# A fused attention and mixture kernel: split pieces and matrix products placed otherwise among the attention steps

## The chip, the cores and the metric

The kernel runs on one core of a Trainium2 chip. The core has a matrix engine (TensorE, PE in the profile, with PEld for its weight loads), VectorE (DVE), ScalarE (ACT), GpSimd (POOL) and SyncE (SP), which issues nearly all DMAs. The metric is the device time of one execution in microseconds, the median of several runs.

## The reference

Three layers run one after the other: local and global attention, a layer that takes the maximum of three products, and a routed mixture with capacity.

```python
s_ll = scale * np.matmul(q_l, k_l.transpose(0, 1, 3, 2))      # 2 x 8 heads, 512 rows, 64 wide, window 32
...
a_l = sm(s_l)
out_l = np.matmul(a_l, np.concatenate([v_g, v_l], axis=2))
...
h = np.maximum(np.maximum(x @ w1, x @ w2), x @ w3)            # 1088 x 512 by 512 x 768
return (h @ w_out).astype(np.float32)
...
expert_idx = np.argmax(logits, axis=1)                        # 8 experts, capacity 288
```

`w1`, `w2`, `w3` and `w_out` arrive as 64-bit floats.

## The kernel before

The whole program is written in a fixed order: each engine works through its own queue in the order in which the source emits instructions, and waits there for what an instruction needs.

**Attention steps.** The local attention is cut into 32 units (`NU`), two for each of 16 sets of a batch, a half and a head pair. The loop `for s in range(-2, NU + 6)` runs a pipeline: in step s the scores of unit s + 2 are multiplied (L179), their mask and maximum are taken on VectorE (L193) and their exponential on ScalarE (L198); unit s is transposed on TensorE (L212) and copied by ScalarE (`ph`, L217); unit s - 1 is multiplied with the values (L226) and scaled by VectorE (`xq`, L228); unit s - 2 is transposed to its place (`pxq`, L234), copied by ScalarE (`xs`, L237), and split into a high and a low part `xh`, `xl` by GpSimd (L239, L240). The string `SEQ` says in which order a step emits these, and where the letters w0 to w2, m0 to m3 and `idle` stand among them. In every fourth step `g_scores` adds the global queries' scores (L257) and `g_copies` takes them out of PSUM (L272).

**Splitting.** `w_stream` turns each 128 x 512 chunk of 64-bit weights into two float32 parts (`wh`, `wl`). There are 18 chunks for the three weights, six groups f of three, and six of `w_out`. A chunk is loaded by SP into a buffer `raww` (L361), of which there are three. Its pieces, in order, are: absolute value on ScalarE (L337), clamp (L339), shift (L342) and sign merge into `ct` (L345) on VectorE, the cast to `wh` on ScalarE (L349), exponent mask (L352) and low part (L354) on VectorE, and two subtractions and additions on GpSimd (L355, L356). `take(ws, n)` emits n pieces; the table `w_steps` gives the number for each step, a third of it at each w. A chunk has seven takes, and the end of one chunk runs in between the start of the next. `load(k + 2)` is emitted when chunk k - 1 has been finished, into the buffer that it leaves.

**Products of the first layer.** `moe_first(f, c0, T)` gives 36 products (L454) of one window of rows with one group f: three maxima of 12 products. `ORDER` lists window, group and the step from which they may run. `pull(n)` emits n of them; `MM` gives the numbers at m0 to m3, 14 in a step. They begin in step 12. What is left of the listed 432 runs after the loop, and everything behind it is a long stretch of products.

**Unread products.** `warm(n)` multiplies a tile of zeros (L88) into a PSUM bank that nobody reads; `idles` gives n for each step.

**Loads.** In even steps the loop issues the next set's queries and keys (`qk`, L97) and values (`rawv`, L101), five buffers each. SP issues in source order, too, and a load that has to wait for its buffer holds the ones behind it.

## Time and profile before

| what | value |
|---|---|
| median of 3 runs | 327.69 us |
| lowest and highest | 327.64 and 328.4 us |
| the profiled execution's own time | 329.9 us |
| its span, first to last instruction | 328.1 us |
| PE busy | 309.8 us, 94% of the span |
| DVE, ACT, POOL busy | 235.7, 181.3, 148.6 us |
| mean granted TensorE clock | 0.974 |

The profiled execution took 2.2 us more than the median, of which 1.8 us lie outside its span. The profile's page gives busy times, 40 slices of the span, and groups of instructions by source line. A group's line reads: line, engine, operation, output from inputs, shapes, count, busy time and mean duration, then the idle time just before and what ended it. The granted clock 1.00 is 2.4 GHz and 0.50 is 1.2 GHz.

### The profile page before, as it was taken

Reading aid. Unit: us, or ns where it says so; the run is one execution under the profiler, and the core shown is the slowest. Engines: PE = TensorE matmul, PEld = TensorE weight load, DVE = VectorE, ACT = ScalarE, POOL = GpSimd, SP = SyncE. Lnnn points to the kernel's source line nnn. Section 1 sums busy time; section 2 is a strip of 40 time slices with the busy share of each in tenths; the row PEclk is TensorE's granted clock in tenths of the full one; section 3 lists DMA queues with packets and bytes.
Section 4 is the critical chain, followed back from the end, with each engine's and each line's share of the span. In section 5 each row is a group of like instructions: output and inputs, shape, how many; then the busy total and the mean of one; then the engine's idle time right before and its main releaser. Section 6 shows DMA issues by size and latency. Waiting matters only on the chain. (4 is left out here: it accounts for less than half of the span.)

```text
span 328.1 us, 8717 instructions
## 1 busy us (share of the span) xinstructions
PE 309.8 (94%) x3280; PEld 264.3 (81%) x3280; DVE 235.7 (72%) x600; ACT 181.3 (55%) x457; POOL 148.6 (45%) x164
## 2 busy tenths in 40 slices
PE   7699868999999999999999999999899999999993
PEld 2355746778887899999999999999799777788762
DVE  2569988796688827998996001765879799999881
ACT  4668477768757522433443121346532689889860
POOL 1128958593674814676888000142000357831131
PEclk9869796999999999999999999999999999999999
DMA  7947777486253962243310011469756189999921
GB/s 243 413 162 274 262 262 249 160 303 212 80 193 125 193 155 66 66 130 128 130 64 3 0 65 64 146 237 346 231 170 256 53 312 399 395 405 399 390 81 32
DMA packets 27656, 64.43 MB, mean 196 GB/s; under 512 B 3018, under 2 KB 8140, under 8 KB 27600
## 3 DMA queue, kind: packets, MB, share of 16 engines
q1 hardware_dynamic: 26304, 59.91, 52.9%
q0 software_dynamic: 1296, 3.82, 3.1%
q8 instruction: 30, 0.49, 0.6%
q14 instruction: 26, 0.21, 0.2%
HBM read 60.95 MB, written 7.27 MB: 208 GB/s over the span
## 5 line engine op out<-in xcount | busy, mean ns | idle before, releaser
L454 PE MATMUL h<-xh,wh 128*128 128x256 f32 (+1 forms) x288 | 85.3, 296 | 0.5 <-DVE hA L441 0.5
L454 PE MATMUL h<-xl,wh 128*128 128x256 f32 (+1 forms) x288 | 85.5, 297 | 0.0
L454 PE MATMUL h<-xh,wl 128*128 128x256 f32 (+1 forms) x288 | 85.5, 297 | 0.0
L454 PEld LDWEIGHTS h<-xh,wh 128*128 128x128 f32 x288 | 55.6, 193 | 1.2 <-DVE hA L441 0.7
L454 PEld LDWEIGHTS h<-xh,wl 128*128 128x128 f32 x288 | 55.9, 194 | 0.8 <-issue 0.7
L454 PEld LDWEIGHTS h<-xl,wh 128*128 128x128 f32 x288 | 55.9, 194 | 0.4 <-issue 0.2
L444 POOL TENSOR_TENSOR hTl<-hA,hTh 128x256 fp32r<-128x256 f32 (+1 forms) x24 | 19.3, 806 | 55.8 <-ACT hTh L443 55.7
L239 POOL CAST xh<-xs 128x128 fp32r<-128x128 f32 x32 | 13.1, 408 | 37.0 <-ACT xs L237 37.0
L859 DVE TENSOR_TENSOR w2l<-rawb,w2h 128x1024 fp32r<-128x1024 f32 x23 | 27.3, 1214 | 2.0 <-ACT w2h L858 2.0
L443 ACT CAST hTh<-hA 128x256 fp32r<-128x256 f32 (+1 forms) x24 | 10.0, 416 | 33.6 <-DVE hA L441 33.5
L739 PE MATMUL x<-hTl,wo_h 128*128 128x256 f32 (+1 forms) x96 | 28.3, 294 | 0.0
L198 ACT ACTIVATE sm<-sm,nm 128x128 f32<-128x128 f32 x64 | 25.3, 399 | 5.3 <-DVE nm L193 5.2
L441 DVE TENSOR_TENSOR hA<-hA,h 128x256 f32<-128x256 f32 (+1 forms) x48 | 20.7, 432 | 10.3 <-PE h L454 8.5
L739 PE MATMUL x<-hTh,wo_l 128*128 128x256 f32 (+1 forms) x96 | 27.9, 291 | 0.0
L739 PE MATMUL x<-hTh,wo_h 128*128 128x256 f32 (+1 forms) x96 | 27.8, 289 | 0.0
L355 POOL TENSOR_TENSOR ct<-ct,wh 128x512 f32<-128x512 f32 x18 | 25.8, 1432 | 1.3 <-DVE ca L352 0.9
L193 DVE CUSTOM_DVE_ANT_0 sm<-s,mask 128x128 f32<-128x128 f32 x64 | 15.9, 285 | 13.8 <-PE s L179 9.2
L942 PE MATMUL py<-w2h,hhl 128*128 128x512 f32 x96 | 25.5, 395 | 0.2 <-DVE idsall L573 0.2
L356 POOL TENSOR_TENSOR wl<-ct,ca 128x512 fp32r<-128x512 f32 x18 | 24.3, 1352 | 2.0 <-DVE ca L354 0.7
L859 DVE TENSOR_TENSOR w1l<-rawb,w1h 128x1024 fp32r<-128x1024 f32 x20 | 23.7, 1216 | 1.7 <-ACT w1h L858 1.6
L858 ACT CAST w2h<-rawb 128x1024 fp32r<-128x1024 f32 x23 | 23.4, 1050 | 1.8 <-DMA rawb<-in_w_dram 1.8
L817 POOL DMA_INDIRECT xg<-x2d,idsall x7 | 14.8, 2120 | 16.0 <-PE xp L829 14.8
(232 smaller groups left out, 723.3 us busy)
## 6 DMA issues: line engine op xcount, KB each, us to landing
rawb<-in_w_dram SPq DMA_DIRECT2D x51, 512.0 KB
raww<-in_w_dram SPq DMA_DIRECT2D x18, 512.0 KB
rawv<-in_v_dram SPq DMA_DIRECT2D x16, 512.0 KB
qk<-in_qk_dram SPq DMA_DIRECT2D x16, 320.0 KB
rawo<-in_w_out_dram SPq DMA_DIRECT2D x6, 512.0 KB
rw<-in_w_dram SPq DMA_DIRECT2D x5, 512.0 KB
out_dram<-zero SPq DMA_DIRECT2D x1, 2176.0 KB
rawg<-in_vo_dram SPq DMA_DIRECT2D x4, 512.0 KB
```

Source lines behind the costliest of these rows:

```text
L193: nc.vector.tensor_tensor_reduce(sm[:, j], ps[:, j, 0:P], mk, scale=-0.125, scalar=3.0e38, op0=ALU.add, op1=ALU.min, accum_out=nm[:, j : j ...
L198: nc.scalar.activation(sm[:, j], sm[:, j], AF.Exp, bias=nm[:, j : j + 1], scale=-1.0, accum_out=ssum[:, j : j + 1])
L355: nc.gpsimd.tensor_tensor(tf, tf, hi.bitcast(F32), op=ALU.subtract)
L356: nc.gpsimd.tensor_tensor(lo, tf, b.bitcast(F32), op=ALU.add)
L441: nc.vector.tensor_tensor(hA[:, :T], hA[:, :T], ph[:, :T], op=ALU.max)
L444: nc.gpsimd.tensor_tensor(hl[:, f_, c0 : c0 + T], hA[:, :T], dst.bitcast(F32), op=ALU.subtract)
L454: nc.tensor.matmul(ph[:, :T], lhsT=w_[:, a], rhs=x_[:, c, c0 : c0 + T], start=n == 0, stop=n == 11)
L739: nc.tensor.matmul(po[:, :T], lhsT=w_[:, f, d * P : (d + 1) * P], rhs=h_[:, f_, c0 : c0 + T], start=k == 0, stop=k == 17)
L817: nc.gpsimd.indirect_dma_start(out=xg[t if j == 0 else j % 2], out_offset=None, in_=src, in_offset=bass.IndirectOffsetOnAxis(ap=IDS[j][0:n ...
L858: nc.scalar.copy(h_, raw_of(j, k))
L859: nc.vector.tensor_tensor(l_, raw_of(j, k), h_.bitcast(F32), op=ALU.subtract)
L942: nc.tensor.matmul(py[0:nt], lhsT=a[:, c, a0 : a0 + nt], rhs=w_[:, c], start=i == 0, stop=i == 23)
```

## The change

All of it lies in the attention steps and the splitting inside them.

- In `split64` the cast to `wh` changes places with the exponent mask, and a chunk's start has three pieces behind the load instead of four. So the cast now comes behind the absolute value of the next chunk, and the low part one take later. The temporaries `ca` and `ct` get three buffers, `raww` five, and chunk k + 3 is loaded when the low part of chunk k - 1 has been emitted.
- Two weight loads are emitted before the loop, and the sets' loads come one set earlier.
- `w_steps` has 2 to 4 pieces in most steps where it had 1 to 7.
- Before step 17, ten products are emitted in a step (`MM`), and the second group's (f = 1) may run from step 14, 16 and 17, its three maxima apart, where they had to wait for step 17. `moe_stream` no longer emits the first product of an entry under the step of the one before.
- `idles` has 26 unread products where it had 12: four as before in step -2, one in each of steps 0 to 11, two in each of steps 12 to 16.
- Three times (sets 0, 2 and 4), half of the global scores is copied by ScalarE instead of VectorE.

```diff
-            (nc.vector.tensor_copy if m < GDVE else nc.scalar.copy)(SG_[b, hp // 2][64 * j : 64 * j + 64, half * 256 : half * 256 + n], o)
+            (nc.vector.tensor_copy if j == 0 and m < GDVE else nc.scalar.copy)(SG_[b, hp // 2][64 * j : 64 * j + 64, half * 256 : half * 256 + n], o)
...
-        b = wp.tile([P, 512], I32, tag="ca", name="ca")
+        b = wp.tile([P, 512], I32, tag="ca", bufs=3, name="ca")
...
-        t = wp.tile([P, 512], I32, tag="ct", name="ct")
+        t = wp.tile([P, 512], I32, tag="ct", bufs=3, name="ct")
...
+        nc.vector.tensor_scalar(a, t, -0x800000, None, op0=ALU.bitwise_and)
+        yield
+
         nc.scalar.copy(hi, tf)
-        yield
-
-        nc.vector.tensor_scalar(a, t, -0x800000, None, op0=ALU.bitwise_and)
         yield
...
-            raw = wp.tile([P, 512, 2], I32, tag="raww", bufs=3, name=name)
+            raw = wp.tile([P, 512, 2], I32, tag="raww", bufs=5, name=name)
...
             next(old, None)
-            if k:
-                load(k + 2)
             yield
-            for _ in range(4):
+            next(old, None)
+            load(k + 3)
+            yield
+            for _ in range(3):
                 next(new, None)
                 yield
...
-    ORDER = [(0, 0, 12), (0, 1, 17), (1, 1, 19), (1, 0, 18), (1, 2, 21), (2, 1, 27), (0, 2, 25), (2, 2, 31), (2, 0, 32), (3, 0, 99), (3, 1, 99), (3, 2, 99)]
+    ORDER = [(0, 0, 12), (0, 1, (14, 16, 17)), (1, 1, 18), (1, 0, 18), (1, 2, (22, 23, 25)), (0, 2, 25), (2, 1, 27), (2, 2, 31), (2, 0, 32), (3, 0, 99), (3, 1, 99), (3, 2, 99)]
...
-    MM = (7, 4, 2, 1)
+    MM = ((5, 3, 2, 0), (7, 4, 2, 1))
...
     dma_v(1)
+    take(ws, 1)
+    dma_qk(3)
+    dma_v(2)
+    take(ws, 1)
...
-            m = (s + 6) // 2
-            if 3 <= m < NSET:
+            m = (s + 8) // 2
+            if 4 <= m < NSET:
                 dma_qk(m)
```

SP's queue at the start, before the change, from the first weight load on (`raww` chunks, `qk` and `rawv` of the sets; the waits are for landed DMAs and for engines that still read the buffer):

```order
L361 DMA raww_164<-in_w_dram 128x1024 [waits DMAHW0_49]
L361 DMA raww_166<-in_w_dram 128x1024 [waits DMAHW1_49]
L97 DMA qk_211<-in_qk_dram 128x640 [waits DMAHW2_49]
L101 DMA rawv_213<-in_v_dram 128x1024 [waits DMAHW3_49]
L361 DMA raww_254<-in_w_dram 128x1024 [waits DMAHW4_49]
L97 DMA qk_299<-in_qk_dram 128x640 [waits DMAHW5_49]
L101 DMA rawv_301<-in_v_dram 128x1024 [waits DMAHW6_49]
L97 DMA qk_389<-in_qk_dram 128x640 [waits DMAHW7_49,PE_49]
L101 DMA rawv_391<-in_v_dram 128x1024 [waits DMAHW0_49]
L361 DMA raww_485<-in_w_dram 128x1024 [waits DMAHW1_49,DVE_49,Activation_49]
```

The same queue after the change:

```order
L361 DMA raww_149<-in_w_dram 128x1024 [waits DMAHW0_49]
L97 DMA qk_151<-in_qk_dram 128x640 [waits DMAHW1_49]
L101 DMA rawv_153<-in_v_dram 128x1024 [waits DMAHW2_49]
L361 DMA raww_155<-in_w_dram 128x1024 [waits DMAHW3_49]
L97 DMA qk_215<-in_qk_dram 128x640 [waits DMAHW4_49]
L101 DMA rawv_217<-in_v_dram 128x1024 [waits DMAHW5_49]
L361 DMA raww_261<-in_w_dram 128x1024 [waits DMAHW6_49]
L97 DMA qk_307<-in_qk_dram 128x640 [waits DMAHW7_49,PE_49]
L101 DMA rawv_309<-in_v_dram 128x1024 [waits DMAHW0_49]
L361 DMA raww_345<-in_w_dram 128x1024 [waits DMAHW1_49]
```

The fourth set's `qk` stands ahead of the second weight chunk instead of behind it, and the fourth chunk's load no longer waits for VectorE and ScalarE.

ScalarE's queue in steps 9 and 10 before the change; `sm` are a unit's exponentials, `ph` the copied transposes that TensorE multiplies next, `wh` the cast of a weight chunk:

```order
L198 ACTIVATE sm_126,ss_541<-sm_126,nm_595 128x128 [waits DVE_49] x2
L201 ACTIVATE ss_541<-ss_541 128x4 [waits Activation_49]
L349 CAST wh_382<-ct 128x512 [waits DVE_49]
L217 COPY ph_650<-pt_647 128x256 [waits PE_49]
L237 COPY xs_665<-pxq_663 128x128 [waits PE_49,Pool_49]
L337 ACTIVATE ca<-raww_254 128x512 [waits DMAHW4_49]
```

The same chunk's cast after the change, in steps 8 and 9:

```order
L337 ACTIVATE ca<-raww_261 128x512 [waits DMAHW6_49]
L198 ACTIVATE sm_125,ss_558<-sm_125,nm_557 128x128 [waits DVE_49] x2
L352 CAST wh_445<-ct 128x512
L272 COPY sg_228<-s_596 64x288 [waits DVE_49,PE_49]
L217 COPY ph_625<-pt_622 128x256 [waits PE_49]
```

The cast stood right behind VectorE's sign merge and waited for it; now it stands behind the next chunk's absolute value and an exponential, and has no wait of its own.

TensorE's queue in step 16 before the change, from its transposes `pt` on (`s` scores, `pv` product with the values, `pxq` transposed result):

```order
L212 MATMUL pt_982<-cst,sm_125 128x128 [waits Activation_49]
L212 MATMUL pt_982<-cst,sm_125 128x128
L179 MATMUL s_987<-qk_800 32x128 [waits DMAHW3_49,DVE_49,PE_49]
L179 MATMUL s_987<-qk_800 32x128 x7
L226 MATMUL pv_1000<-rawv_685,ph_939 32x64 [waits DVE_49]
L226 MATMUL pv_1000<-rawv_685,ph_939 32x64 x7
L234 MATMUL pxq_1011<-cst,xq_962 128x128 [waits Activation_49]
```

The same step after the change:

```order
L212 MATMUL pt_1016<-cst,sm_125 128x128 [waits Activation_49]
L212 MATMUL pt_1016<-cst,sm_125 128x128
L179 MATMUL s_1021<-qk_699 32x128 [waits DMAHW2_49,DVE_49,PE_49]
L179 MATMUL s_1021<-qk_699 32x128 x7
L226 MATMUL pv_1034<-rawv_594,ph_958 32x64 [waits DVE_49]
L226 MATMUL pv_1034<-rawv_594,ph_958 32x64 x7
L234 MATMUL pxq_1045<-cst,xq_981 128x128 [waits Activation_49]
L88 LDWEIGHTS idle
L88 MATMUL warm<-idle 32x512 [waits PE_49]
L454 MATMUL h_0_0_1007<-xl,wh_801 128x256
```

Two unread products and ten products `h` of the first layer now follow each step's `pxq`, where steps 15 and 16 had neither.

## Rows read from the trace of the kernel before

**Rows 1.** The page's second part: busy tenths of 40 slices of 8.2 us.

```profile
PE   7699868999999999999999999999899999999993
PEclk9869796999999999999999999999999999999999
```

**Rows 2.** Stretches cut at step starts: us, busy of each engine, PEclk, DMA, GB/s.

```profile
4.05:11.63 7.58, 6.05 (x142) 3.17 (x141) 3.81 (x25) 4.46 (x20) 0.00 (x0) 1.00 1.01 374
11.63:15.22 3.59, 1.50 (x36) 0.81 (x36) 1.85 (x9) 3.33 (x14) 1.54 (x4) 0.92 1.00 400
15.22:21.85 6.63, 6.62 (x90) 3.36 (x91) 2.83 (x14) 2.29 (x8) 0.74 (x2) 0.53 0.70 273
21.85:34.75 12.90, 11.02 (x240) 6.30 (x241) 11.82 (x45) 10.31 (x43) 10.02 (x16) 1.00 0.59 213
34.75:52.70 17.95, 13.52 (x237) 10.35 (x237) 14.88 (x44) 11.78 (x44) 13.81 (x17) 0.89 0.71 237
52.70:58.57 5.87, 5.87 (x65) 4.98 (x66) 5.70 (x16) 4.30 (x16) 5.28 (x6) 0.50 0.98 339
58.57:98.67 40.10, 39.87 (x742) 33.81 (x742) 29.86 (x114) 28.99 (x107) 25.76 (x40) 0.99 0.54 184
```

**Rows 3.** The same view, cut where the granted clock is low.

```profile
14.60:21.40 6.80, 6.18 (x88) 3.21 (x88) 2.54 (x14) 2.77 (x11) 1.18 (x3) 0.50 0.77 303
35.10:38.50 3.40, 3.40 (x36) 2.97 (x29) 2.91 (x9) 2.53 (x10) 3.26 (x4) 0.50 0.64 234
52.20:59.00 6.80, 6.30 (x81) 5.24 (x81) 6.20 (x20) 4.95 (x17) 6.13 (x7) 0.50 0.98 348
```

**Rows 4.** Waits of PE, first 60 us: total us, times, longest.

```profile
PE pt L212 <- ACT ph L217: 2.5, 3, 1.2
PE s L179 <- DVE nm L193: 2.2, 3, 1.0
PE pt L212 <- DVE ca L352: 1.6, 1, 1.6
PE s L179 <- DMA qk<-in_qk_dram: 1.4, 1, 1.4
```

**Rows 5.** Waits of ACT from 4 to 60 us, the same columns.

```profile
ACT wh L349 <- DVE ct L345: 6.9, 4, 2.6
...
ACT ca L337 <- DMA raww<-in_w_dram: 1.2, 1, 1.2
```

**Rows 6.** Waits of SP's DMA queue, first 60 us.

```profile
SPq L361 <- DVE ca L354: 41.0, 7, 12.0
```

**Rows 7.** Timeline of SP's queue: start us, duration, what is issued.

```profile
11.75 0.33 SPq L101 DMA_DIRECT2D rawv<-in_v_dram  x1
24.11 0.33 SPq L361 DMA_DIRECT2D raww<-in_w_dram  x1
```

**Rows 8.** Groups by line on DVE, 11 to 23 us: busy us, mean ns.

```profile
L272 DVE COPY sg<-s 64x256 f32<-64x256 f32 x2 | 0.8, 420 | 0.0
...
L345 DVE SCALAR_TENSOR_TENSOR ct<-raww,ca 128x512 int32<-128x512 int32 x1 | 0.7, 681 | 0.0
L342 DVE TENSOR_SCALAR ca<-ca 128x512 int32<-128x512 int32 x1 | 0.5, 468 | 0.0
```

**Rows 9.** The same on DVE, 23 to 41 us.

```profile
L342 DVE TENSOR_SCALAR ca<-ca 128x512 int32<-128x512 int32 x3 | 3.5, 1153 | 0.0
...
L345 DVE SCALAR_TENSOR_TENSOR ct<-raww,ca 128x512 int32<-128x512 int32 x3 | 2.7, 901 | 0.0
```

**Rows 10.** The same on POOL, 23 to 41 us.

```profile
L355 POOL TENSOR_TENSOR ct<-ct,wh 128x512 f32<-128x512 f32 x3 | 4.4, 1479 | 0.0
```

**Rows 11.** Timeline of PE in step -2, the four unread products.

```profile
4.55 1.04 PE L88 MATMUL warm<-idle 128*32 128x512 bf16 x4
```

**Rows 12.** Timeline of PE in step 19, two products in a row.

```profile
62.65 0.28 PE L454 MATMUL h<-xh,wh 128*128 128x256 f32 x1
...
62.77 0.28 PE L454 MATMUL h<-xl,wh 128*128 128x256 f32 x1
```

More of the change, by code (lines that the diff above doesn't have):

```diff
@@ L359, in dma_w @@
         if wide:
-            raw = wp.tile([P, 512, 2], I32, tag="raww", bufs=3, name=name)
+            raw = wp.tile([P, 512, 2], I32, tag="raww", bufs=5, name=name)
             nc.sync.dma_start(raw.rearrange("p n t -> p (n t)"), src.bitcast(I32))
         else:
-            raw = wp.tile([P, 512], F32, tag="raww", bufs=3, name=name)
+            raw = wp.tile([P, 512], F32, tag="raww", bufs=5, name=name)
             nc.sync.dma_start(raw, src)
@@ L367, in split32 @@
     def split32(raw, *to):
-        for _ in range(4):
+        for _ in range(5):
             yield
@@ L371, in split32 @@
         nc.scalar.copy(hi, raw)
-        yield
         yield
@@ L390, in w_stream @@
         load(2)
+        yield
         old = iter(())
@@ L399, in w_stream @@
             next(old, None)
-            if k:
-                load(k + 2)
             yield
-            for _ in range(4):
+            next(old, None)
+            load(k + 3)
+            yield
+            for _ in range(3):
                 next(new, None)
@@ L580, in tile_block @@
     WIN1 = [(0, 256), (256, 256), (512, 288), (800, 288)]
-    ORDER = [(0, 0, 12), (0, 1, 17), (1, 1, 19), (1, 0, 18), (1, 2, 21), (2, 1, 27), (0, 2, 25), (2, 2, 31), (2, 0, 32), (3, 0, 99), (3, 1, 99), (3, 2, 99)]
+    ORDER = [(0, 0, 12), (0, 1, (14, 16, 17)), (1, 1, 18), (1, 0, 18), (1, 2, (22, 23, 25)), (0, 2, 25), (2, 1, 27), (2, 2, 31), (2, 0, 32), (3, 0, 99), (3, 1, 99), (3, 2, 99)]
     def moe_stream():
         for g, f, at in ORDER:
+            at = at if isinstance(at, tuple) else (at if at < 99 else 99 + f / 10,) * 3
+            k = 0
+            yield at[0]
             for _ in moe_first(f, *(WIN1[g])):
-                yield at if at < 99 else 99 + f / 10
+                k += 1
+                if k < 36:
+                    yield at[k // 12]
     class Stream:
@@ L602, in tile_block @@
     GDVE = 6
-    MM = (7, 4, 2, 1)
-    w_steps = {-2: 1, 1: 2, 2: 1, 3: 2, 4: 2, 5: 1, 6: 2, 7: 1, 8: 1, 9: 1, 10: 6, 11: 5, 12: 5, 13: 3, 14: 2, 15: 3, 16: 7, 17: 3, 18: 1, 19: 5, 20: 4, 21: 3, 22: 1, 24: 4, 26: 6, 27: 3, 28: 1, 29: 1, 30: 5, 31: 4, 32: 2, 33: 2}
-    idles = {-2: 4, 0: 1, 4: 3, 6: 1, 9: 1, 10: 1, 11: 1}
+    MM = ((5, 3, 2, 0), (7, 4, 2, 1))
+    w_steps = {1: 1, 2: 2, 3: 3, 4: 2, 5: 2, 6: 3, 7: 2, 8: 3, 9: 2, 10: 3, 11: 3, 12: 4, 13: 4, 14: 4, 15: 4, 16: 4, 17: 3, 18: 2, 19: 3, 20: 3, 21: 3, 22: 2, 23: 3, 24: 3, 25: 3, 26: 2, 27: 3, 28: 2, 29: 2, 30: 4, 31: 3, 32: 3}
+    idles = {-2: 4, 0: 1, 1: 1, 2: 1, 3: 1, 4: 1, 5: 1, 6: 1, 7: 1, 8: 1, 9: 1, 10: 1, 11: 1, 12: 2, 13: 2, 14: 2, 15: 2, 16: 2}
     GQ = {17: (0, 0), 21: (0, 1), 28: (1, 0), 31: (1, 1)}
@@ L647, in tile_block @@
             elif c_[0] == "m" and c_ != "max":
-                pull(MM[int(c_[1])])
+                pull(MM[s > 16][int(c_[1])])
         if s % 2 == 0:
-            m = (s + 6) // 2
-            if 3 <= m < NSET:
+            m = (s + 8) // 2
+            if 4 <= m < NSET:
                 dma_qk(m)
-            if 2 <= m - 1 < NSET:
+            if 3 <= m - 1 < NSET:
                 dma_v(m - 1)
```

## The prediction

> **What bounds the kernel now.** I read the slices of the page first: PE is at nine tenths or more from about 60 us to the end, and below that only in the first quarter, which is also where the granted clock drops [rows 1]. Everything behind the attention steps is one stretch of products, so a change in the first 60 us is worth what it brings forward the point from which PE runs without a gap, plus the PE work that it moves ahead of that point. It keeps that worth to the end, since PE's queue has no later idle time of any size to give it back in.
>
> I then cut the first 100 us at the starts of steps (the scores of unit s + 2 on PE) [rows 2]: steps -2 to 2, step 3, steps 4 and 5, 6 to 11, 12 to 16, step 17, 18 to 29. In the last of these PE is busy 39.87 of 40.10 us, 3.34 us a step. Before, it is not: in steps 6 to 16 (21.85 to 52.70 us) PE is busy 24.5 of 30.9 us, while VectorE is busy 26.7. There the splitting sets the pace, and unevenly. The waits of PE say through whom: 4.1 us for ScalarE's `ph` and for the transposes that come behind VectorE's mask piece, 2.2 us for the maximum `nm` on VectorE, 1.4 us for the load of a `qk` [rows 4]. ScalarE itself waited 6.9 us for the sign merge in front of its cast `wh`, with `ph` queued behind it [rows 5].
>
> Three more things cost time. The clock is at its low level, 1.2 GHz, in three stretches, together 17.0 us [rows 3]; each comes behind steps in which PE stood still. SP's queue stood 41.0 us on `raww` buffers [rows 6], once from 11.75 to 24.11 us, with no load issued [rows 7]. And VectorE's pieces are longer when GpSimd works: the shift takes 0.47 us alone and 1.15 us on average between 23 and 41 us, the sign merge 0.68 and 0.90 [rows 8, 9].
>
> **The change part by part.** All terms are differences in the one profiled execution (329.9 us, span 328.1). I take them off the median, 327.69 us, since that execution's extra 2.2 us are mostly outside its span.
>
> *Steps -2 to 3.* The first chunk's load is ahead of the fourth set's `qk`, but the second is no longer. A chunk is 512 KB, and at this stretch's 400 GB/s [rows 2] that is 1.3 us. PE waited 1.4 us for this `qk` at the end of step 3 [rows 4], and ScalarE 1.2 us for the first `raww` [rows 5], which the change asks for one step later. I take the smaller end, **-1.3**; nothing less than 0 and at most -2.6 (both waits in a row).
>
> *Steps 4 and 5.* They took 6.63 us at a clock of 0.53 [rows 2]. The six steps behind them took 2.15 each at full clock with VectorE as the limit. Two such steps and 0.3 for the global scores that fall in step 5 are 4.6: **-2.0** if the clock stays up. What keeps it up is that PE no longer stands 1.4 us before step 4, and has an unread product in each of steps 1 to 3; four of those took 1.04 us, so one costs about 0.22 us [rows 11]. The other end is 0.
>
> *Steps 6 to 11.* Both tables give 16 takes, so the same pieces. Before, ten of the sixteen were in steps 10 and 11 and ran over into step 12. Now they run in their own steps. VectorE was busy 11.82 of 12.90 us [rows 2]; that is the lower end, and 14.5 the upper, if one more chunk's stretch of VectorE and GpSimd (about a step) falls here. Three more unread products are 0.66 us of PE time, hidden behind VectorE as long as it is the limit. I take 13.2: **+0.3**.
>
> *Steps 12 to 16.* 20 takes before and after, but four in each step instead of 5, 3, 2, 3, 7, and no backlog at the start. PE was busy 13.52 us of 17.95 [rows 2]. It gets 14 products more at 0.12 us each (62.65 to 62.77 us [rows 12]), 1.7 us, and ten unread ones, 2.2 us, and loses about half of the 3.4 us at low clock [rows 3], 1.7 us: 15.7, the lower end. The upper end is the old 17.95. VectorE's work, 14.88 us busy, is the same. The cast now finds its input ready, so that `ph` doesn't stand behind it; that is a part of the 4.1 us. What is late next is VectorE itself. I take 16.4, nearer to what PE and VectorE need: **-1.5**.
>
> *Step 17.* It took 5.87 us at a clock of 0.50 [rows 2]; a step like it took 3.34 at full clock, 3.5 with the global scores. Against that stands a new wait: the third maximum of group 1 comes in this step, and its last weight chunk is finished by pieces emitted at the step's start, with a VectorE piece and two of GpSimd at 1.48 us [rows 10] to run. The products stand in PE's queue ahead of step 18's transposes and scores. I take 0.8 us for it, between 0 and 3.5: **-1.6**.
>
> *From step 18 on.* Where 36 products were done before step 17, now 50 are: 14 fewer behind it, in a stretch where PE is the limit, 14 x 0.12 = **-1.7**. The pieces per step (2 to 4) fit in beside 3.34 us of PE. The same number is done at the end of step 32, so the rest of the splitting starts from the same place, and the loads are one chunk earlier.
>
> *Hidden.* Three copies of 0.42 us move from VectorE to ScalarE [rows 8], beside VectorE's other half; ScalarE was busy 10.31 of 12.90 us in steps 6 to 11 and carries it. If it didn't, it would be 1.3 us. The extra buffers take SP's waits away; the loads were not waited for after step 3, so I count nothing for that.
>
> The sum is -1.3 - 2.0 + 0.3 - 1.5 - 1.6 - 1.7 = -7.8: **319.9 us**.
>
> **The rivals.** *The clock falls anyway.* If the steps that VectorE paces leave PE too idle, the stretches at 15 and 52 us come back, and steps 4, 5 and 17 take as long as before. Without -2.0 and -1.6 the sum is -4.2: 323.5. For it: three stretches in 45 us before [rows 3], and a step's own products alone don't fill it. Against it: steps 6 to 11 held 1.00 with three unread products in six steps [rows 2], and now there is one in each. The Trainium skill's page "TensorE: Matmul & The Clock Gate" (section "Part 4: PE-mode transpose") says that transposes do not count for the clock like other work; by that rule steps full of transposes would go this way. The steps from 6 to 11 in the trace, two transposes and a third in each, held the clock, so it gets no more than the chance below.
>
> *VectorE and GpSimd stop each other everywhere.* If a piece waits for a running GpSimd instruction, spreading makes every piece meet one. The excess of the two dearest is 0.69 and 0.22 us [rows 8, 9], 0.9 us a chunk, for the 1.3 chunks that ran undisturbed before: +1.2. And if the two are a single resource, steps 6 to 16 gain nothing (+0.3 and -1.5 become 0): -1.3 - 2.0 + 1.2 - 1.6 - 1.7 = -5.4, 322.3 us. The page "SBUF — State Buffer" of the Trainium skill (section "SBUF: two separate sides") has this as a full exclusion for whole instructions, in VectorE's fast modes or with two inputs there. The trace agrees in size, since 0.47 becomes 1.15, but on average over three only.
>
> *PE becomes the limit already in step 12.* Then steps 6 to 11 go to 11.8 (-1.1), steps 12 to 16 to 15.7 (-2.3), step 17 to 3.5 (-2.4): -1.3 - 2.0 - 1.1 - 2.3 - 2.4 - 1.7 = -10.8, 316.9 us.
>
> *Products ahead of their weights: slower.* In steps 15, 16 and 17 the three maxima of group 1 start one step, or less, after their chunk's last pieces are emitted. If GpSimd lags by a step, each first product on a low part holds PE's whole queue, attention included, for one VectorE piece and two GpSimd instructions, about 0.7 + 2 x 1.4 = 3.5 us. Three of them are 10.5, of which 0.8 is counted: -7.8 + 9.7 = +1.9, 329.6 us. It decides from about 2.6 us each on. Against it: the chunks of steps 15 and 16 are complete a step and more before.
>
> *It does not do what it says:* the waits only move, and 14 more unread products (3.0 us) stand in PE's way: -4.2 + 3.0 = -1.2, 326.5 us.
>
> **How the numbers follow.** The forecast 0.52; clock 0.14; exclusion 0.10; PE the limit 0.12; slower 0.07; no effect 0.05. The range 316.0 to 324.5 takes in the first four with their ends, and leaves out the slower ones and a little of each tail. A measurement of this kernel tells 0.3%, 1.0 us, from no change. All of the first four are faster by more, and most of the last, whose spread reaches into no change; the slower rival is above it nearly always. Faster 0.88, same 0.05, slower 0.07.
>
> **What would show it.** Right: step 4 starts at about 13.9 us, step 12 at about 31.8, step 17 at about 48, step 18 at about 52, and PE's waits for `ph` and for the mask piece shrink below 1.5 us; ScalarE's wait in front of its cast is gone; SP issues loads between 12 and 24 us; the granted clock is 1.00 over most of 14 to 60 us. Wrong: low-clock stretches with the unread products between them (the first rival), shifts above 1.1 us in all stretches with step starts as before (the second), or PE waiting for GpSimd's `wl` in steps 15 to 17 (the slower one).

## The result and the profile after

The changed kernel takes 333.06 us (median of four runs, 331.03 to 333.1) beside 327.81 us for the kernel before (327.64 to 328.4): a ratio of 1.0143, 95% interval 1.0103 to 1.0184. A second set (g1 below) gave 331.78 beside 327.93 us, 1.0178 (1.0087 to 1.0268). The forecast, 319.9 us and a range to 324.5, was wrong, in its sign too. The profiled execution has 333.07 us and a span of 331.3, 3.2 us more than the one before.

The slices of the page, now of 8.3 us each, PE busy and granted clock in tenths, against [rows 1]:

```profile
PE   7988897999997899999999999999999999999974
PEclk9997799999999799999999999999999999999999
```

The first quarter is little fuller than before, and there is a new dip in the 13th and 14th slices, just behind 100 us, with a low clock in the 14th. Cut at starts of steps as in [rows 2], with the columns of that view; the stretches are here steps -2 to 3, 4 and 5, 6 to 11, 12 to 16, 17, and 18 to 28:

```profile
4.05:14.10 10.05, 8.75 (x179) 4.20 (x178) 4.50 (x31) 6.88 (x30) 0.74 (x2) 1.00 1.01 377
14.10:18.11 4.01, 3.89 (x89) 2.21 (x88) 3.48 (x16) 2.85 (x15) 1.82 (x4) 1.00 1.03 408
18.11:34.49 16.38, 12.31 (x240) 6.93 (x241) 13.39 (x45) 12.79 (x49) 10.88 (x16) 0.90 1.03 402
34.49:52.51 18.02, 18.02 (x262) 12.53 (x262) 16.05 (x45) 11.34 (x44) 14.56 (x18) 0.91 0.72 246
52.51:57.96 5.45, 3.59 (x66) 2.93 (x65) 3.59 (x13) 4.03 (x13) 4.93 (x7) 1.00 0.65 220
57.96:95.15 37.19, 36.72 (x673) 30.61 (x672) 27.50 (x104) 27.72 (x103) 21.99 (x33) 1.00 0.47 161
```

Step 6 starts at 18.11 us instead of 21.85, 3.7 us earlier. By step 12 (34.49 against 34.75) nearly all of it is gone. The low-clock stretches have moved rather than gone; three answer to [rows 3], and the third is at a place where there was none before:

```profile
25.94:29.35 3.41, 3.41 (x60) 2.32 (x54) 2.10 (x10) 1.81 (x8) 0.87 (x2) 0.50 1.03 404
36.18:39.59 3.41, 3.41 (x48) 2.28 (x39) 3.17 (x5) 1.04 (x5) 3.25 (x4) 0.50 0.52 169
111.27:114.68 3.41, 3.41 (x17) 3.38 (x16) 1.51 (x2) 0.34 (x2) 2.81 (x4) 0.50 0.23 84
```

PE's waits in the first 60 us, against [rows 4]. Those for the mask piece and the `qk` load are gone and that for `ph` is down from 2.5 to 0.8, as foreseen; a wait for GpSimd's `wl` is new. (The wait for the load is not gone in every execution: in g2, which has the same instructions up to step 29, PE waited twice 0.9 us for a `qk`.)

```profile
PE h L456 <- POOL wl L356: 1.9, 1, 1.9
PE s L179 <- DVE nm L193: 1.7, 1, 1.7
PE s L179 <- issue: 1.6, 1, 1.6
...
PE pt L212 <- ACT ph L217: 0.8, 1, 0.8
```

ScalarE no longer waits for the merge in front of its cast (6.9 us in [rows 5]); now it waits for the maxima. SP stands 8.5 us on the raw buffers, 41.0 in [rows 6]:

```profile
ACT sm L198 <- DVE nm L193: 6.0, 5, 3.1
```

```profile
SPq L361 <- DVE ca L354: 8.5, 4, 3.8
```

So the change did to loads and casts what it says. To see where steps 7 to 9 lose the gain, VectorE, GpSimd and PE from the timeline (start us, duration):

```profile
22.11 1.45 DVE L342 TENSOR_SCALAR ca<-ca 128x512 int32<-128x512 int32 x1
23.59 1.64 DVE L345 SCALAR_TENSOR_TENSOR ct<-raww,ca 128x512 int32<-128x512 int32 x1
25.16 0.28 DVE L193 CUSTOM_DVE_ANT_0 sm<-s,mask 128x128 f32<-128x128 f32 x1
```

```profile
22.00 1.28 POOL L355 TENSOR_TENSOR ct<-ct,wh 128x512 f32<-128x512 f32 x1
23.36 1.33 POOL L356 TENSOR_TENSOR wl<-ct,ca 128x512 fp32r<-128x512 f32 x1
```

```profile
25.80 0.64 PE L179 MATMUL s<-qk 64*32 64x128 f32 x16 [1.70 <-DVE nm L193]
```

The shift ends 0.28 us behind GpSimd's first operation and the merge 0.54 us behind its second; alone they took 0.47 and 0.68 us in all [rows 8]. The maxima that step 9's scores need stand behind both, PE stands 1.7 us for them, and then the clock falls (25.94 us). The fall does not have to follow: in e3 and g1 below PE stood the same 1.7 us there, and the clock stayed at 1.00. In front of step 12's scores PE stands 1.6 us more (34.49 us). The view calls it "issue", but the scores start 0.1 us behind a maximum (ended at 34.39), ahead of which a merge and a mask piece took 1.55 and 1.38 us beside GpSimd; before, the same place had 1.25 us.

The other loss is late. Up to 95 us the steps keep 0.5 us of gain; the 341st product, in the stretch without attention, starts at 121.87 us before and 124.32 after. In between (PE's timeline, after):

```profile
106.75 0.43 PE L226 MATMUL pv<-rawv,ph 128*32 128x64 f32 x16 [1.21 <-DVE xq L228]
...
109.97 0.65 PE L305 MATMUL gpv<-rawg,gph 128*32 128x64 f32 x32 [1.47 <-ACT xs L237]
```

In the trace of before, PE goes from the products into these two weighted sums without a gap (105.44 and 107.05 us). Now it stands 2.7 us, and the products behind run at the low clock, 0.24 us apart instead of 0.13. It is not that products are missing in front of the sums: in both traces 14 stand in PE's queue between the weighted sum before and this `pv`, and eight between `pv` and `gpv`. What is late is what the sums wait for. VectorE in the changed kernel:

```profile
102.60 0.45 DVE L443 TENSOR_TENSOR hA<-hA,h 128x288 f32<-128x288 f32 x1 [1.34 <-POOL xh L239]
...
103.42 1.39 DVE L342 TENSOR_SCALAR ca<-ca 128x512 int32<-128x512 int32 x1
104.85 1.65 DVE L345 SCALAR_TENSOR_TENSOR ct<-raww,ca 128x512 int32<-128x512 int32 x1
106.42 0.28 DVE L228 TENSOR_TENSOR xq<-pv,ss 128x128 f32<-128x128 f32 x1
```

A maximum of the products (`hA`, L443) stands first. VectorE is idle for 1.34 us ahead of it, since it reads what ScalarE's copy of `hA` wrote at 102.09 to 102.51 us, and the clamp, the shift and the merge of the next chunk stand behind. GpSimd's two operations run from 103.05 to 105.95 us, the shift and the merge take 1.39 and 1.65 us, and `xq`, for which PE stands 1.21 us, comes last. ScalarE has the cast of the next finished maximum in front of `xs`, waits 2.8 us for it on VectorE, and so is late for `gpv`. Before, no maximum stood there, and `xq` came ahead of the merge:

```profile
104.40 0.28 DVE L228 TENSOR_TENSOR xq<-pv,ss 128x128 f32<-128x128 f32 x1
104.60 1.57 DVE L345 SCALAR_TENSOR_TENSOR ct<-raww,ca 128x512 int32<-128x512 int32 x1
```

The last loss is in the tail, where PE waits for nothing that the profile shows, in the middle of the last unit's products:

```profile
322.22 0.85 PE L1031 MATMUL acc<-rawb,x 128*32 128x256 f32 x12 [1.84 <-issue]
```

### The profile page after: what moved, and what is told of

Its sections match the earlier page's. It is cut to its first block, busy times and chain, and to the rows that moved or that the text cites. A ratio compares the mean times of both kernels' runs of the same rounds, so it can differ in the third digit from the quotient of the medians.

```text
span 331.3 us, 8752 instructions
## 1 busy us (share of the span) xinstructions
PE 312.0 (94%) x3294; PEld 264.0 (80%) x3294; DVE 234.7 (71%) x597; ACT 182.7 (55%) x460; POOL 146.8 (44%) x164
## 5 line engine op out<-in xcount | busy, mean ns | idle before, releaser
L443 DVE TENSOR_TENSOR hA<-hA,h 128x256 f32<-128x256 f32 (+1 forms) x48 | 20.7, 431 | 10.8 <-PE h L456 9.2
L239 POOL CAST xh<-xs 128x128 fp32r<-128x128 f32 x32 | 14.1, 440 | 31.7 <-ACT xs L237 31.7
L355 POOL TENSOR_TENSOR ct<-ct,wh 128x512 f32<-128x512 f32 x18 | 24.7, 1375 | 5.2 <-ACT wh L352 4.8
```

The source lines that it names most:

```text
L355: nc.gpsimd.tensor_tensor(tf, tf, hi.bitcast(F32), op=ALU.subtract)
L443: nc.vector.tensor_tensor(hA[:, :T], hA[:, :T], ph[:, :T], op=ALU.max)
```

## The experiments

Times are medians; the ratio is to the kernel before in the same set, with its 95% interval. Runs of one kernel spread by several us, with the granted clock: 25 runs of the kernel before in one set went from 324.93 us at a mean clock of 0.989 to 331.85 at 0.971. The letters e to h are four sets; the kernel before had medians of 326.74, 327.95, 327.93 and 328.71 us in them, so between sets the medians of two kernels can differ by 1 to 2 us for that alone, and there the ratios and their intervals are compared.

**e1: the low part on VectorE.** In `split64`:

```
-        nc.gpsimd.tensor_tensor(tf, tf, hi.bitcast(F32), op=ALU.subtract)
-        nc.gpsimd.tensor_tensor(lo, tf, b.bitcast(F32), op=ALU.add)
+        nc.vector.tensor_tensor(tf, tf, hi.bitcast(F32), op=ALU.subtract)
+        nc.vector.tensor_tensor(lo, tf, b.bitcast(F32), op=ALU.add)
```

> The changed kernel with the last two operations of a chunk's split (the subtraction and the sum that give wl) on VectorE instead of GpSimd. Theory A (the steps 7 to 11 gave the early gain back because VectorE's pieces run beside GpSimd's and each is held up by the other: in the changed kernel the shift took 1.45 us and the merge 1.64 us in the step at 22.3 us, with GpSimd's two operations of 1.28 and 1.33 us beside them, against 0.45 and 0.68 alone): the shift falls to about 0.47 us and the merge to about 0.7 in all stretches, steps 8, 9 and 11 take 2.2 to 2.5 us instead of 3.4 to 3.7, step 12 starts 2 us or more earlier than at 34.5 us, the wait of the products for wl in step 17 (1.9 us) shrinks below 0.5, and the time is 328 to 330 us. Rival B (the pieces stand in a bad order in VectorE's queue, ahead of the maxima, whatever GpSimd does): VectorE gets about 1.4 us more work a chunk, steps 7 to 16 become longer by 0.7 us or more each, and the time is 335 us or above.

338.42 us, 1.0339 (1.0258 to 1.0419). VectorE's pieces of a chunk, by line, 18 to 46 us, in the changed kernel:

```profile
L345 DVE SCALAR_TENSOR_TENSOR ct<-raww,ca 128x512 int32<-128x512 int32 x4 | 6.3, 1566 | 0.0
...
L342 DVE TENSOR_SCALAR ca<-ca 128x512 int32<-128x512 int32 x4 | 3.3, 834 | 0.0
L349 DVE TENSOR_SCALAR ca<-ct 128x512 int32<-128x512 int32 x4 | 2.8, 709 | 0.0
L354 DVE SCALAR_TENSOR_TENSOR ca<-raww,ca 128x512 f32<-128x512 uint32 x4 | 2.7, 683 | 0.0
...
L339 DVE TENSOR_SCALAR ca<-ca 128x512 f32<-128x512 f32 x4 | 1.9, 470 | 0.0
```

and in e1:

```profile
L355 DVE TENSOR_TENSOR ct<-ct,wh 128x512 f32<-128x512 f32 x5 | 4.0, 796 | 1.8 <-ACT wh L352 1.8
L354 DVE SCALAR_TENSOR_TENSOR ca<-raww,ca 128x512 f32<-128x512 uint32 x5 | 3.4, 678 | 0.0
...
L345 DVE SCALAR_TENSOR_TENSOR ct<-raww,ca 128x512 int32<-128x512 int32 x4 | 2.8, 701 | 0.0
L356 DVE TENSOR_TENSOR wl<-ct,ca 128x512 fp32r<-128x512 f32 x4 | 2.8, 692 | 0.1
L339 DVE TENSOR_SCALAR ca<-ca 128x512 f32<-128x512 f32 x4 | 2.1, 533 | 0.0
L349 DVE TENSOR_SCALAR ca<-ct 128x512 int32<-128x512 int32 x4 | 1.8, 460 | 0.0
L342 DVE TENSOR_SCALAR ca<-ca 128x512 int32<-128x512 int32 x4 | 1.7, 434 | 0.0
```

The sums of the means are 4.26 us a chunk in the changed kernel and 4.29 in e1, with two operations more. So theory A holds for the pieces. It holds for the early steps as well: step 12 starts at 31.91 us instead of 34.49, steps 8, 9 and 11 take 1.74, 2.45 and 2.13 us, although step 7 takes 3.47. The wait for `wl` in step 17 went to 0.9 us, not below 0.5. It falls on the whole time. Behind 120 us VectorE, which there has the maxima of the products too, is behind with the split of the last weights, and PE waits 3.2 us for `wo_h` and 2.6 us for `hA`.

**e2: thirteen products a step.**

```
-    MM = ((5, 3, 2, 0), (7, 4, 2, 1))
+    MM = ((5, 3, 2, 0), (6, 4, 2, 1))
```

> The changed kernel with 13 products a step instead of 14 from step 17 on, so that those listed ahead of the end of the steps last as long as they did in the kernel before; all else as changed. Theory C (the 4.7 us lost between 95 and 124 us come from the products running out one step early: nothing stands between the transposes, the weighted sums and the global products of the last steps, PE stands 3.5 us and its clock falls once): the wait of PE ahead of the global weighted sums (1.5 us) and the low-clock stretch at 111 us go away, and the time is 329.5 to 331 us. Rival D (the loss there comes from the weight pieces, four in step 30 and three in 31 and 32, or from the loads that come earlier): PE's waits there stay above 2.5 us and the time is 332.5 to 333.5 us.

327.19 us, 0.9993 (0.9957 to 1.0028): 5.9 us under the changed kernel by the medians of two sets, 1.5% (4.9 us) by the ratios, more than theory C asked. Step 18 starts at 58.01 us as in the changed kernel (57.96); the 341st product starts at 119.13 instead of 124.32. PE's waits from 88 to 126 us are down to one, and the low-clock stretch behind 111 us is gone:

```profile
PE pt L212 <- ACT ph L217: 0.5, 1, 0.5
```

The time is theory C's, its reason is not: with 13 a step, 13 products instead of 14 stand in front of `pv` and seven instead of eight in front of `gpv`, and PE waits less. The clamp, the shift and the merge ran at 99.13 to 100.71 us, ahead of GpSimd's two operations (from 101.64 us on), with `xq` right behind and the maximum later. Rival D falls too, as the pieces and the loads are those of the changed kernel.

**e3: the products as before**, `ORDER`, `moe_stream` and `MM` put back:

```
-    ORDER = [(0, 0, 12), (0, 1, (14, 16, 17)), (1, 1, 18), (1, 0, 18), ...
+    ORDER = [(0, 0, 12), (0, 1, 17), (1, 1, 19), (1, 0, 18), ...
-    MM = ((5, 3, 2, 0), (7, 4, 2, 1))
+    MM = (7, 4, 2, 1)
```

> The changed kernel with the products in the order and numbers of the kernel before (36 in steps 12 to 14, none in 15 and 16, 14 from step 17); splitting, casts, buffers, loads and unread products as changed. Theory C: the late loss is gone whole and so is the wait for wl in step 17 (1.9 us), against the 1.7 us of PE work that was done ahead; the clock is lower in 46 to 58 us since the steps 15 and 16 are emptier (up to 2 us); 328.5 to 331 us. If the products' new places were worth what I had counted (1.7 us from step 18, and a part of step 17), undoing them would instead make it slower: 334.5 us or above.

325.53 us, 0.9968 (0.9924 to 1.0011). The late loss and the wait for `wl` are gone; step 17 takes 3.33 us. At the change's numbers the new places of the products were worth less than nothing. The profile is of the fastest of ten runs (323.24 us, clock 1.00).

**e4: all three tables as before**, but without the take at step -2, since the change makes two ahead of the steps. `ORDER`, `moe_stream` and `MM` as in e3, `idles` as in f3, and

```
-    w_steps = {1: 1, 2: 2, 3: 3, ...
+    w_steps = {1: 2, 2: 1, 3: 2, 4: 2, 5: 1, 6: 2, ...
```

> The changed kernel with all three tables (products, weight steps, unread products) as before: what is left of the change is the cast behind the mask piece, the third temporaries, five raw buffers, the loads that stand earlier and the three copies on ScalarE. Theory A and C together (the tables lose, the rest gains): step 6 still starts 1 us or more earlier than the kernel before, no loss after 95 us, 326 to 327.5 us, at or under the kernel before. Rival E (the early loads or the order inside the split lose): 330 us or above.

333.64 us, 1.0187 (1.0113 to 1.0261). Neither theory: the changed split ends a chunk one take later, and the take that I left out makes two. PE waited 7.7 us for `wl` in four places. It says only that the old table without that take does not fit the new split; the loads are tried by themselves in f4.

**f4: the loads alone.** On the kernel before:

```
-            raw = wp.tile([P, 512, 2], I32, tag="raww", bufs=3, name=name)
+            raw = wp.tile([P, 512, 2], I32, tag="raww", bufs=5, name=name)
...
-            if k:
-                load(k + 2)
+            load(k + 3)
...
+    take(ws, 1)
+    dma_qk(3)
+    dma_v(2)
+    take(ws, 1)
```

> The kernel before with the loads of the change alone: five raw buffers, each chunk loaded one turn earlier, the first two chunks and the fourth set asked for ahead of the steps; casts, temporaries and the three tables as before. Theory F (the early gain, step 6 at 18.1 instead of 21.9 us, comes from the loads: PE no longer stands before step 4 and the clock does not fall there): step 6 starts at 18 to 19 us and the low-clock stretch at 14.6 to 21.4 us is gone, without the unread products of steps 1 to 3; if VectorE's busy steps 10 to 13 do not take it back, the time is 3 us below the kernel before, ratio 0.988 to 0.993. Rival G (the unread products and the spread pieces hold the clock): the low-clock stretch at 15 us stays and the time is within 1 us of the kernel before.

326.31 us, 0.9939 (0.9911 to 0.9967). Step 6 starts at 18.57 us: theory F holds there, without the unread products of steps 1 to 3. But the clock falls later instead. Step 13 starts at 38.66 us against 39.27, so of a lead of 3.3 us 0.6 is left there:

```profile
31.48:38.31 6.83, 6.09 (x50) 4.40 (x51) 6.30 (x17) 4.13 (x17) 6.59 (x6) 0.50 0.87 312
48.55:55.38 6.83, 6.05 (x92) 4.28 (x89) 5.75 (x18) 4.69 (x17) 6.17 (x7) 0.50 0.63 209
```

**f3: products and unread products as before.** e3 with

```
-    idles = {-2: 4, 0: 1, 1: 1, 2: 1, 3: 1, 4: 1, ..., 11: 1, 12: 2, 13: 2, 14: 2, 15: 2, 16: 2}
+    idles = {-2: 4, 0: 1, 4: 3, 6: 1, 9: 1, 10: 1, 11: 1}
```

> The changed kernel with the products and the unread products as before (12 unread instead of 26); splitting, casts, buffers and loads as changed. Against the changed kernel with the products alone put back (325.5 us). Theory H (the unread products stand where PE waits for VectorE anyway and cost nothing, and the clock does not hang on them): the same step starts within 0.5 us to step 18, and the same time within 1 us. Rival I (they hold the clock): two or more low-clock stretches between 14 and 60 us, and 328 us or more. Rival J (they stand in PE's way in steps 12 to 16, 0.2 us each): 1.5 to 2.5 us faster.

328.17 us, 1.0006 (0.9965 to 1.0046), 2.6 us above e3 by the medians, 0.4% by the ratios, whose intervals overlap: the time alone does not decide. The clock does. The median granted clock of ten runs is 0.970 here and 0.990 in e3, and it is low for 17 us in this profile, where that of e3 has no such stretch in its first 300 us. So theory H falls, rival I holds:

```profile
26.59:40.24 13.65, 13.65 (x170) 8.12 (x157) 8.86 (x35) 7.36 (x29) 8.78 (x12) 0.50 0.81 308
53.89:57.31 3.42, 3.42 (x56) 2.87 (x39) 3.42 (x11) 2.86 (x10) 3.26 (x5) 0.50 0.44 133
```

**f1: e3 with the low part of the first six chunks on VectorE.**

```
+        eng = nc.vector if to[0] == "w" and to[1] < 2 else nc.gpsimd
...
```

The subtraction and the sum are then `eng.tensor_tensor`.

> The changed kernel with the products as before, and the last two operations of the split of the first six chunks on VectorE instead of GpSimd. Theory A (VectorE and GpSimd hold each other up; VectorE spends no more time when it does the work itself, 4.3 us a chunk either way, and the maxima do not stand behind long pieces): step 12 starts at 31 to 32 us instead of 32.9, step 18 at 51 to 52 instead of 53, and the time is 1 to 2 us under the one with the products alone put back, 323.5 to 324.5 us. Rival K (with the products put back the splitting no longer sets the end of step 17): the same within 0.7 us.

325.36 us, 0.9933 (0.9898 to 0.9968); the median as e3's. Rival K. Steps 6 to 11 took 14.29 us instead of 15.43, both at full clock, but the clock fell in step 17.

**f2: e2 with the same.**

> The changed kernel with 13 products a step from step 17 on, and the last two operations of the split of the first six chunks on VectorE. Theory A and C together: the gain of step 6 is kept to step 18 (at 54 us instead of 58), the late loss stays away: 323 to 324.5 us. If the new wait for wl in step 17 is moved rather than removed: 325 to 327 us.

325.47 us, 0.9928 (0.9881 to 0.9975), 1.7 us under e2 by the medians, 0.65% by the ratios, whose intervals overlap. 323 to 324.5 was expected, and 325 to 327 if the wait for `wl` is only moved; it was. Step 18 started at 57.07, not 54 us: a low-clock stretch of 6.8 us lay over steps 8 and 9, and step 17 still took 5.01, with waits of 0.9 us for `wl`, now on VectorE, and 0.6 us for ScalarE's copy of the global scores.

**g1: the changed kernel again.**

> The changed kernel itself, unaltered, beside the kernel before on the same chip as the three others of this set. If the 333 us of its first four runs are the kernel's own time: 331 to 334 us, PE's waits of 1.2 and 1.5 us ahead of the last weighted sums and the wait of 1.9 us for wl in step 17 in the profile again, whatever the number of low-clock stretches. If they were three low-clock stretches that fell by chance: 328 to 330 us and the waits smaller.

331.78 us. All the waits are there (1.9, 1.2, 1.5), with one low-clock stretch in the first 120 us instead of three, and none behind the two late waits. From step 29 to the 341st product it took 27.60 us, against 29.17 in the first profile and 26.20 before: about half of the late loss is the clock.

**g2: fewer products from step 30 on alone.**

```
-    MM = ((5, 3, 2, 0), (7, 4, 2, 1))
+    MM = ((5, 3, 2, 0), (7, 4, 2, 1), (6, 3, 2, 1))
...
-                pull(MM[s > 16][int(c_[1])])
+                pull(MM[(s > 16) + (s > 29)][int(c_[1])])
```

> The changed kernel with 14 products a step up to step 29 and 12 from step 30 on: nothing is altered before 95 us, and the listed products last to the end of the steps. Theory C (the products run out ahead of the last step): the wait ahead of the global weighted sums (1.5 us) and the low-clock stretch at 111 us go away, and 3 to 5 us of the changed kernel's time are back: 328 to 330 us, as with 13 a step (327.2). Rival L (13 a step helped in steps 18 to 29, as the profile of that run shows 2.1 us gained there, and not at the end): 331 us or more.

328.74 us, 1.0038 (0.9989 to 1.0087): 3.0 us under the changed kernel of the same set, and nothing is altered ahead of 95 us: rival L falls. Between 88 and 126 us PE waits only here:

```profile
PE pt L212 <- ACT ph L217: 1.1, 1, 1.1
```

Twelve products stand in front of `pv`, the fewest of all, and seven in front of `gpv`, so theory C's reason falls here again. VectorE now has the maximum behind the pieces and behind `xq`:

```profile
103.31 0.69 DVE L345 SCALAR_TENSOR_TENSOR ct<-raww,ca 128x512 int32<-128x512 int32 x1
104.11 0.29 DVE L228 TENSOR_TENSOR xq<-pv,ss 128x128 f32<-128x128 f32 x1
...
104.90 0.44 DVE L443 TENSOR_TENSOR hA<-hA,h 128x288 f32<-128x288 f32 x1
```

Of all profiles, the wait in front of `gpv` is in those three alone that have 14 products a step and 50 of them done by step 17 (the changed kernel, g1, e1). In them 246 products precede unit 31's transposes, and the maximum after the first 240 comes just ahead of the pieces; elsewhere it is 229 to 244. e1 parts the two waits: with the maximum at the same place but GpSimd's two operations gone, shift and merge take 0.57 and 0.69 us there and the wait in front of `pv` is 0.3 us instead of 1.2; the one in front of `gpv`, for `xs` behind the cast of the finished maximum, stays at 1.5. That the maximum's place does the rest is read from these rows; no run moved it alone.

**g3: e2, and the last third of (0, 1) a step later.**

```
-    ... (0, 1, (14, 16, 17)), ...
+    ... (0, 1, (14, 16, 18)), ...
```

> 13 products a step, and the last 12 products of f 0, group 1 released in step 18 instead of 17; else as changed. Theory M (in step 17 the products stand ahead of their weights: PE waits 1.8 us for wl, with the attention of step 18 queued behind): that wait goes away, step 17 takes 3.4 to 3.7 us instead of 5.3, and the time is 1 to 2 us under the one with 13 a step alone, 325.2 to 326.2 us. Rival N (GpSimd and VectorE are a step late there, so the wait moves to the maxima or to step 18): the same within 0.5 us.

325.89 us, 0.9976 (0.9948 to 1.0005), and all ten runs within 325.24 to 326.73: theory M. Step 17 takes 3.03 us instead of 5.30; step 18 then takes 3.52 instead of 2.77.

**g4: e2 without unread products in steps 12 to 16.**

```
-    idles = {..., 11: 1, 12: 2, 13: 2, 14: 2, 15: 2, 16: 2}
+    idles = {..., 11: 1}
```

> 13 products a step, and no unread products in steps 12 to 16, where the changed kernel has two a step; one a step stays in steps 0 to 11. In steps 14 to 16 of the changed kernel PE was busy all of 3.14 us a step, 0.54 of them with two unread products. Theory O (PE is the limit there, and the unread products are in its way): these steps take 2.7 to 2.9 us, and the time is 1 to 2.5 us under 327.2. Rival P (VectorE, busy 2.7 to 3.1 us a step there, is the limit as much, or the clock falls without them): within 0.7 us, or slower with a low-clock stretch between 40 and 60 us.

328.38 us, 1.0044 (0.9999 to 1.0088), not faster than e2 (0.9993, 0.9957 to 1.0028), with a median clock of 0.978 against 0.990: rival P. Steps 14 and 15 are shorter, 2.42 and 2.41 us, as theory O has it, but step 17 takes 6.15, and the clock is low from 27.47 to 37.71 and, behind step 17, from 58.19 to 61.60 us.

**h1: e3 with eleven more unread products.**

```
-    6: 1, 7: 1, 8: 1, 9: 1, 10: 1, 11: 1
+    6: 1, 7: 3, 8: 4, 9: 2, 10: 3, 11: 4
```

> The changed kernel with the products as before and eleven more unread products: 3, 4, 2, 3 and 4 in the steps 7 to 11 instead of one each, where PE stands still for VectorE's maxima. Theory Q (the give-back in steps 7 to 13 is in good part the clock: a low-clock stretch of 3.4 us costs 1.7, and more unread products in a time in which PE waits anyway keep it up): no low-clock stretch between 20 and 45 us, steps 7 to 11 as long as in the run with the products alone put back (13.7 us together), and 324 to 325 us with less spread. Rival R (they come in front of the scores and so delay the chain to VectorE): steps 7 to 11 longer by 0.2 us for each, 326.5 us or more.

325.18 us, 0.9904 (0.9859 to 0.9949). Steps 7 to 11 take 13.74 us, in e3 13.73: they cost nothing (rival R falls), and no clock falls between 20 and 45 us. The ratio is below e3's (0.9968), with overlapping intervals; the median clock is 0.997 against 0.990.

**h2: g3 with the same eleven.**

> 13 products a step, the last group of f 0 released in step 18, and the eleven more unread products in steps 7 to 11. Theory Q: the low-clock stretch at 26.5 us of the run without them goes, step 13 starts at 36 to 37 us instead of 37.9, 323.8 to 324.8 us against 325.9. Rival R: 326.5 us or more.

324.8 us (324.49 to 325.34), 0.987 (0.9834 to 0.9906): theory Q, and the lowest median and ratio of all. Steps 7 to 11 and 12 to 16 in g3:

```profile
20.11:34.75 14.64, 10.61 (x206) 5.79 (x206) 12.41 (x39) 11.40 (x42) 10.40 (x15) 0.88 1.03 401
34.75:52.26 17.51, 16.62 (x261) 11.57 (x262) 16.11 (x45) 11.30 (x44) 13.97 (x17) 1.00 0.74 254
```

and in h2, with step 17:

```profile
19.85:33.58 13.73, 11.58 (x216) 5.80 (x216) 12.52 (x39) 11.23 (x42) 9.83 (x14) 1.00 1.03 403
33.58:51.06 17.48, 16.62 (x261) 11.57 (x261) 15.89 (x45) 11.31 (x44) 14.54 (x18) 1.00 0.80 283
51.06:54.10 3.04, 2.92 (x62) 2.40 (x62) 3.00 (x13) 2.60 (x8) 2.68 (x4) 1.00 0.35 100
```

**h3: g3 with the low part of the first six chunks on VectorE**, by the line of f1.

> 13 products a step, the last group of f 0 released in step 18, and the last two operations of the split of the first six chunks on VectorE instead of GpSimd. Theory A (GpSimd's two operations cost VectorE about as much as they take, and stand in front of the maxima for longer): steps 7 to 13 together 1 to 1.5 us shorter, 324.4 to 325 us against 325.9. Rival: VectorE's time is the same either way, so the same within 0.5 us, or longer when the clock falls in the longer step 7.

325.9 us, 0.9881 (0.9815 to 0.9947), three runs from 323.73 to 326.39 and one of 328.7. The median is g3's, the ratio about 1% lower and within h2's interval: undecided. In the profile steps 7 to 12 took 15.72 us, in h2 16.86 with the clock full in both, so the pair on GpSimd costs about 1.1 us there. It was lost again in step 17, 5.01 us instead of 3.04 at full clock: the two operations, now in VectorE's queue (51.67 to 53.09 us), stand ahead of the step's maxima, and step 18's scores wait. The clock falls behind that:

```profile
54.34 0.45 PE L179 MATMUL s<-qk 64*32 64x128 f32 x16 [1.94 <-ACT sg L272]
```

**h4: the loads with the new table of unread products.**

> The kernel before with the loads of the change and its table of unread products (26 instead of 12); casts, temporaries, splitting and products as before. If the loads and the unread products are what is good in the change: the low-clock stretches at 31.5 to 38.3 and 48.6 to 55.4 us of the loads alone shrink to one or none, and the time is 1 to 2.5 us under 326.3, as low as or below the changed kernel with its products put back (325.5). If spreading the pieces and the casts matter: within 0.7 us of 326.3 or above.

326.17 us, 0.9922 (0.9887 to 0.9956), as the loads alone (0.9939): the second of the two expected outcomes. One low-clock stretch instead of two, but a wait of 1.1 us in the tail that f4 has not.

## Why the prediction was wrong

Step 4 started where I had it (14.1 us, 13.9 forecast); steps 12, 17 and 18 did not (34.5, 52.5 and 58.0 us for 31.8, 48 and 52). By the terms of the sum, from the starts of the steps in the two profiled executions:

| stretch | forecast | before | after | came out |
|---|---|---|---|---|
| steps -2 to 3 | -1.3 | 11.17 | 10.05 | -1.1 |
| steps 4, 5 | -2.0 | 6.63 | 4.01 | -2.6 |
| steps 6 to 11 | +0.3 | 12.90 | 16.38 | +3.5 |
| steps 12 to 16 | -1.5 | 17.95 | 18.02 | +0.1 |
| step 17 | -1.6 | 5.87 | 5.45 | -0.4 |
| step 18 to the 341st product | -1.7 | 63.30 | 66.36 | +3.1 |
| from there to the end | 0 | 206.25 | 206.97 | +0.7 |

*The base.* I took 7.8 us off the median, holding that the profiled execution's extra 2.2 us lay outside its span. They did not: time less span is 1.8 us before (329.9 and 328.1) and 1.8 after (333.07 and 331.3). It was an execution at a low mean clock, 0.974, where other runs had up to 0.989. So the terms that live on low-clock stretches, -2.0 and -1.6, were probably in part in the median already. This alone is 2.1 us of the miss of 13.2: the profiles differ by 3.2 us, the medians by 5.3. The 0.3% that I took for the uncertainty of a measurement was too little as well: the intervals above reach 0.3 to 0.9% to either side.

*Steps -2 to 5: right in size, wrong in one reason.* I gave the unread products credit for the clock in steps 4 and 5. f4 has none in steps 1 to 3 and starts step 6 at 18.57 us all the same; the loads did it.

*Steps 6 to 11: mis-sized.* I took 13.2 us and gave 14.5 as the upper end; it took 16.4. (Of the sixteen takes eleven, not ten, had been in steps 10 and 11; no term hangs on it.) About 1 us is the clock: e3, with the same instructions up to step 11 and no low stretch, took 15.43. The other 2.2 are VectorE's work and its order; half of it, 1.1 us, went with GpSimd's two operations (f1, 14.29), and the rest was not told apart. The shift and the merge meet GpSimd's two operations of the chunk ahead, and cost 834 and 1566 ns on average instead of the 468 and 681 of [rows 8]. Since two of them stand together in front of a maximum, PE waits for their sum, and in this profile its clock then falls, so that the first and second rival came in part, together. I had the price of a piece beside GpSimd in [rows 9, 10] and spread it as an average instead of putting it in front of the maxima. On the exclusion, the Trainium skill's page "SBUF — State Buffer" (section "SBUF: two separate sides") says that one of the two engines holds the shared port for a whole instruction and the other blocks. The trace agrees, as far as spans of GpSimd tell it: the two pieces in front of the maxima that step 9 waits for each ended 0.3 to 0.5 us behind a GpSimd operation, and e1, with these operations taken off GpSimd, has them at 434 and 701 ns.

*Steps 12 to 16: mis-sized.* 18.0 instead of 16.4, of which 0.5 us is the clock (17.48 in h2 with the clock full). PE and VectorE are both near their limit: in h2 they are busy 16.62 and 15.89 of the 17.48 us. My lower end, 15.7, had PE's busy time of before less half of its low-clock loss; an unread product there takes 0.27 us, not 0.22, and ten of them are 2.7. Leaving them out shortens these steps (16.82 us in g4, 18.07 in e2), but step 17 gets longer, the clock lower, and the time no less.

*Step 17: the new wait mis-sized.* Booked at 0.8 us, it was 1.9. The text's slower rival had three such waits, and one came. g3 takes it out by one step's delay, and step 17 goes to 3.03 us, below the 3.5 that I took for a full step.

*From step 18 on: the step that failed.* "In a stretch where PE is the limit, 14 fewer products, nothing later gives it back." The term was -1.7 us and came out at +3.1. I took PE to be the limit up to the end of the list, so that a product done early was time saved. But every twelve products also give ScalarE a copy or VectorE a maximum, and the last twelve of a three a cast. With 50 done ahead, these came in other places among the last attention steps: a maximum stood ahead of VectorE's shift and merge, these ran beside GpSimd's operations with `xq` behind both, `xq` and `xs` were late, PE stood 2.7 us in front of two weighted sums that it had reached without a gap before, and the clock was low for 3.4 us. e2 and g2 show that it hangs on the products: with 13 a step, or with 12 in the last steps alone, the two waits and the low-clock stretch are gone, and 4.9 us (e2, by the ratios) and 3.0 us (g2, in one set) come back. That GpSimd makes most of the first wait is shown by e1; that the place of the maxima makes the second is read from the rows and not tested by itself. In e2 the stretch from step 18 to the 341st product is 61.1 us instead of 63.3, so the term's -1.7 was there to be had.

*The tail*, 1.8 us of wait, was not foreseen, and its cause stays open (below).

The ratio of h2, 0.987, is what is left of the change when these are mended: two of its numbers altered (13 instead of 14 products, 18 instead of 17) and eleven unread products more. The loads alone give 0.9939 (0.9911 to 0.9967). What the spread splitting and the new casts bring by themselves was not told apart from the spread of the runs.

## What to carry over

Work that is moved forward on a busy engine takes with it what it triggers on the others: before you count it as time saved, look at what then stands ahead of the short operations for which the busy engine waits, up to the last of them. Where an engine waits for another's short reduction, put the dearest pieces ahead of that reduction into the sum one by one, not as an average. And take the base from an execution with the same mean clock as the runs that you forecast; time less span shows how much lies outside the span.

## What the runs showed of the hardware that I had not expected

- Taking two operations over from GpSimd cost VectorE no time of its own between 18 and 46 us: 4.29 us a chunk against 4.26 (e1). What it can cost is their place in its queue (step 17 in h3).
- Unread products in a wait of PE were free (steps 7 to 11 took 13.74 us with eleven more in h1, 13.73 in e3), and the clock followed them: 14 fewer took the median granted clock of ten runs from 0.990 to 0.970 (e3, f3), ten fewer from 0.990 to 0.978 (e2, g4), while the kernel before had 0.983 to 0.984 in all these sets. In the time this shows less clearly, 0.4% and 0.5% with intervals that overlap.
- PE's wait "issue" in the last unit goes with their number: with 12 unread products 0 to 0.6 us (before, f4, e4, f3), with 16 it was 0.9 (g4), with 26 or 37 from 1.1 to 1.9. f3 and e3, and f4 and h4, differ in nothing else. Why is open; no run tested it.
